# Scaling and transposing the next pair's queries one slot later, in a fused retention and feed-forward kernel

## The chip, the cores and the metric

The kernel runs on one core of a Trainium2 chip. The metric is device time in microseconds (us) of one execution; lower is better. Every engine (TensorE or PE, VectorE or DVE, ScalarE or ACT, GpSimd or POOL, SyncE or SP) has its own queue and works through it strictly in order; semaphores join them.

## The reference

Two blocks, one after the other, in float32.

```python
# retention: batch 4, 8 heads, 768 steps, head size 64
for t in range(S):
    state = gamma * state + k[:, :, t] (outer) v[:, :, t]
    y[:, :, t] = scale * q[:, :, t] @ state
x = y.transpose(0, 2, 1, 3).reshape(3072, 512)
# feed-forward: w_in 512 x 2048, w_out 2048 x 512 (given as float64)
h = x @ w_in
g = h * erf(softplus(h))
out = g @ w_out
```

## The kernel before

**Tokens.** The 3072 tokens are cut into 24 chunks of 128 (`j`), two to a group (`g`, 12 groups, `NG`). A *pair* is the two chunks `a = 2g+2` and `b = 2g+3`. Retention of a chunk is done in closed form: `begin` multiplies keys by queries (L566) and keys by values (L573) on PE, `states` masks and adds on DVE (L582, L593), `results` multiplies with states and values on PE (L611, L622) and copies to `xT` on ACT (L630), `crossed_sums` adds the rest on DVE (L641). `split_x` cuts a group's `xT` into three float32r parts, `x_hi` on ACT (L314), `x_lo` and `x_dif` on DVE (L315, L316).

**Preparing a pair.** Before a pair can begin, `load_pair` loads its values and keys (`v`, `kn`; four DMAs issued by POOL) and, in another layout, its keys and queries (`kb`, then `qb`; 16 DMAs each on SP, 128-byte rows). `prepare` is a generator of five steps:

1. DVE transposes `kb` into `kT` (L543),
2. DVE multiplies `qb` by the query scales (L538),
3. DVE transposes `qb` into `qT` (L543),
4. ACT scales the eight heads of the first chunk's `v` (L550, eight instructions),
5. ACT scales the eight heads of the second chunk's `v` (L550, eight more).

`(steps, prep, n)` runs the next `n` of them.

**Periods and slots.** From group 3 on, a period `g` has eight slots. In each slot PE computes one `pair_unit` (L720): a tile of 128 columns of `h` for two groups, 8 matmuls into a bank `a` (parts hi and lo) and then 4 into a bank `b` (part dif). Two pairs of banks take turns, `o0`/`o1` and `o2`/`o3`. The order of the work is written out by hand in `period`: one dictionary says what PE does ahead of a slot's unit (`begin` of both chunks ahead of slot 2, `results` ahead of slot 5), another what the other engines do in a slot, and `put` comes last in it: ACT copies bank `a` into `h` (L322), DVE adds bank `b` (L323), POOL stores `h` to memory (`hids`, L731). So a unit of slot n+2 can write its bank `a` only after L322 of slot n, and its bank `b`, two thirds into the unit, only after L323 of slot n.

**Conversion.** w_out comes as float64 words and is turned into float32 on DVE and ACT, piece by piece. POOL loads quarters of a piece into `raw` (L208), then a piece has five steps: `power` from the exponents (L230, and L1019 on ACT at the end of the slot), L244, L249, L253 (after it `raw` is free), L265 (after it POOL stores the piece, `wof`, L271). `(convert, n)` runs the next `n` steps.

**Buffers.** Nearly all of these tiles (`kb`, `qb`, `kT`, `qT`, `v`, `kn`, `xT`, `w`, `power`) come out of one pool of 34 equal buffers, `b4`; a load waits until the buffer that it was given is free. `h` and the masked scores `am` share a pool of six buffers, `b2`, so ACT can write an `h` only when the store of the `h` that last held its buffer has ended.

**After the periods** (groups 10 to 12 and the loop over `project`, L905) come the gate and the second product; their own order does not change.

The slots of a period as they stand in the loop:

Of the kernel before, what the change touches and what calls it, by code (L numbers as in the profile page):

```python
# [49 lines left out]
def kernel(  # L50
# [19 lines left out]
    NG = B * S // GT  # L70
# [460 lines left out]
    def prepare(j):  # L531


        for name, store, x in (("k", KT, KB[j]), ("q", QT, QB[j])):
            if name == "q":
                own = x.rearrange("p u (a d) -> p u a d", d=32)
                scale = kq_b[:, 1, :, j % NC : j % NC + 2].rearrange("p u c a -> p u (c a)")
                nc.vector.tensor_tensor(  # L538
                    own, own, scale[:, :, :, None].to_broadcast([P, HP, 8, 32]), op=ALU.mult
                )  # L540
                yield
            t = b4(name + "T", [HP, 2 * C])
            nc.vector.transpose(t.rearrange("p u t -> p (u t)"), x.rearrange("p u t -> p (u t)"))  # L543
            for i in range(2):
                store[j + i] = t[:, :, i * C : (i + 1) * C]
            yield
        for i in range(2):
            for h in range(H):
                x = V[j + i][:, h]
                nc.scalar.activation(x, x, AF.Copy, scale=kq_s[:, (j + i) % NC, 0, h : h + 1])  # L550
            yield
# [245 lines left out]
    prep = prepare(JPC + 2)  # L797
# [127 lines left out]
    def joined(at, to, g):  # L925

        a, b = 2 * g + 2, 2 * g + 3
        return {
            at: [(begin, a, ps_h), (begin, b, ps_r)],
            to: [(results, a, None, ps_h), (results, b, None, ps_r)],  # L930
        }
# [4 lines left out]
    def period(g, prep, next_prep):  # L936

        a, b = 2 * g + 2, 2 * g + 3
        one, two = partial(partial, unit), partial(partial, pair_unit)
        if g == G2:  # L940
            units = [one(g, n) for n in range(NPC // 2)]
            return units, {0: [(results, a), (results, b, None, ps_h)]}, {
                0: [(crossed_sums, a), (crossed_sums, b)],
                1: [(split_x, a, 2)],
                2: [(split_weights, 4)],
                3: [(steps, next_prep, 4)],
            }, range(4)
        if g < NG:
            units = [two(g - 1, ft) for ft in range(8 * (g % 2), 8 * (g % 2) + 8)]
        if g == G2 + 1:  # L950
            return units, joined(2, 5, g), {
                0: [(steps, prep)],
                1: [(split_weights, 5)],
                2: [(states, a), (states, b)],
                3: [(split_weights, 6)],
                4: [(split_weights, 7)],
                5: [(crossed_sums, a), (crossed_sums, b)],
                6: [(split_x, a, 2)],
                7: [(steps, next_prep, 4)],
            }, range(4)  # L960
        if g < NG - 2:
            return units, joined(2, 5, g), {
                0: [(steps, prep), (convert, 1)],
                1: [(convert, 2)],
                2: [(states, a), (convert, 1)],
                3: [(states, b), (convert, 1)],
                4: [(convert, 2 if g < 8 else 1)],
                5: [(crossed_sums, a), (crossed_sums, b)],
                6: [(split_x, a, 2)],
                7: [(steps, next_prep, 4)],  # L970
            }, LOADS.get(g, ())
        if g == NG - 2:
            return units, {1: [(begin, a)], 2: [(results, a)], 3: [(begin, b)], 5: [(results, b)]}, {
                0: [(steps, prep), (load_w_out, 0)],
                1: [(states, a), (load_w_out, 1)],
                2: [(crossed_sums, a), (split_w_out, 0)],
                3: [(states, b), (split_x, a)],
                4: [(split_w_out, 1), (load_hiddens, 0)],
                5: [(crossed_sums, b)],
                6: [(split_x, b), (softplus, 0), (load_w_out, 2)],  # L980
                7: [(erf, 0), (gated, 0)],
            }, ()
        if g == NG - 1:
            return units, {}, {
                0: [(split_g, 0), (split_w_out, 2), (load_w_out, 3)],
                1: [(split_g, 1), (load_hiddens, 1)],
                2: [(split_w_out, 3)],
                3: [(softplus, 1), (load_w_out, 4)],
                4: [(erf, 1)],
                5: [(split_w_out, 4), (load_w_out, 5)],  # L990
                6: [(gated, 1)],
                7: [(split_g, 2), (load_hiddens, 2)],
            }, ()
        return [one(NG - 1, n) for n in range(NPC // 2)], {}, {
            0: [(split_w_out, 5), (load_w_out, 6)],
            1: [(split_g, 3), (load_w_out, 7)],
            2: [(split_w_out, 6)],
        }, ()

    for g in range(G2, NG + 1):  # L1000
        pair = load_pair(2 * g + 4) if 2 * g + 4 < NJ else iter(())
        next_prep = prepare(2 * g + 4) if 2 * g + 4 < NJ else iter(())
        units, pe, other, loads = period(g, prep, next_prep)
        for i, work in enumerate(units):
            for f, *args in pe.get(i, ()):
                f(*args)
            put = work()
            steps(pair, 3)
            for part in itertools.islice(quarters, loads.count(i)):
                load_quarter(part)  # L1010
            if g == NG - 1 and i % 2:
                W.pop(NPC // 2 + i // 2)
            if g == NG:
                W.pop(i)
            for f, *args in other.get(i, ()):
                f(*args)
            put()
            while behind:
                behind.pop(0)()  # L1019
        prep = next_prep  # L1020
    split_w_out(7)

    for n in range(NG * NU):
        g, i = divmod(n, NU)
# [62 lines left out]
```

## Time and profile before

| What | Value |
|---|---|
| median of the runs | 614.31 us (614.19, 614.31, and one of 3471.9) |
| the profiled execution | 614.87 us, of it a span of 613.2 us in the profile |
| PE busy | 605.6 us, 99% of the span |
| DVE busy | 459.6 us, 75% |
| ACT busy | 390.6 us, 64% |
| POOL busy | 131.8 us, 21% |
| granted TensorE clock | full speed |
| chain that ended last | PE 98% |

Times in rows of the profile are in us from the start of the span. In a timeline a row gives start, duration, engine, line, operation, output and input, count, and in brackets how long the engine stood idle before it and what released it. In the chain of waits a row gives start, duration and what the end waited on at that time. The period of group 4 begins about 128 us into the span, that of group 9 about 261 us.

### The profile page before, as it was taken

How to read it: one execution, taken by the hardware profiler on the slowest of the kernel's cores; microseconds unless marked ns; L12 is line 12 of the kernel's file. 1: busy time of each engine (PE TensorE's matmuls, PEld its weight loads, DVE VectorE, ACT ScalarE, POOL GpSimd, SP SyncE). 2: the span in 40 equal slices, each digit the busy share in tenths (PEclk: the TensorE clock that was granted, in tenths of full speed). 3: DMA queues.
4: the chain of work that ended last, by engine and by line, in shares of the span. 5: the costliest groups of instructions: out<-in, count | busy, mean ns of one | idle time of the engine just before them, and what ended most of it. 6: DMA issues, size and time to landing. Idle time of an engine off the chain costs nothing.

```text
span 613.2 us, 13161 instructions
## 1 busy us (share of the span) xinstructions
PE 605.6 (99%) x5222; PEld 507.8 (83%) x5222; DVE 459.6 (75%) x581; ACT 390.6 (64%) x614; POOL 131.8 (21%) x228
## 2 busy tenths in 40 slices
PE   8999999999999999999999999999999999999997
PEld 7888889888888788888888988888888888888886
DVE  5899978796968779787758978686786768668640
ACT  3667446354451635435387699879789888988920
POOL 1086335443526255242112100000000000000000
PEclk9999999999999999999999999999999999999999
DMA  9999659977889896878435934325324333531300
GB/s 204 321 268 267 158 133 253 250 153 230 208 242 235 233 289 162 260 177 263 163 133 191 288 131 129 128 87 172 103 78 163 104 117 125 171 114 59 104 35 34
DMA packets 143949, 106.28 MB, mean 173 GB/s; under 512 B 103056, under 2 KB 123792, under 8 KB 143888
## 3 DMA queue, kind: packets, MB, share of 16 engines
q1 hardware_dynamic: 128160, 58.09, 37.0%
q0 software_dynamic: 15168, 47.21, 23.9%
q8 instruction: 41, 0.67, 0.5%
q10 hardware_dynamic: 560, 0.14, 0.1%
q14 instruction: 20, 0.16, 0.1%
HBM read 69.75 MB, written 35.65 MB: 172 GB/s over the span
## 4 chain that ended last, share of the span: by engine, by line
PE 98%; DMA 0%; DVE 0%; ACT 0%; issue 0%; DVEq 0%
PE o L720 31%; PE o L905 21%; PE r L905 11%; PE hp L905 11%; PE hp L665 9%; PE o L693 3%; PE hp L566 1%; PE hp L720 1%; PE r L720 1%; PE r L566 1%; PE r L611 1%; PE r L622 1%; PE r L573 1%; PE hp L611 1%; PE r L465 1%; PE o L504 1%
## 5 line engine op out<-in xcount | busy, mean ns | idle before, releaser
L322 ACT ACTIVATE h<-o 128x512 f32<-128x512 f32 x74 | 44.0, 597 | 100.7 <-PE o L720 84.1
L720 PE MATMUL o<-x_hi,w_hi 128*128 128x512 f32 x272 | 108.1, 397 | 0.0
L720 PE MATMUL o<-x_lo,w_lo 128*128 128x512 f32 x272 | 106.0, 390 | 0.0
L860 DVE TENSOR_TENSOR e<-hid,e 128x1024 f32<-128x1024 f32 x48 | 56.7, 1222 | 61.8 <-ACT e L850 61.8
L720 PE MATMUL o<-x_dif,w_dif 128*128 128x512 f32 x272 | 73.0, 390 | 1.3 <-DVE h L323 1.3
L323 DVE SCALAR_TENSOR_TENSOR h<-o,h 128x512 f32<-128x512 f32 x74 | 50.3, 682 | 27.5 <-ACT h L322 21.1
L731 POOL DMA_DIRECT2D hids<-h x72 | 39.3, 546 | 146.3 <-DVE h L323 125.5
L720 PEld LDWEIGHTS o<-x_dif,w_dif 128*128 128x128 f32 x272 | 50.9, 188 | 12.7 <-DVE h L323 2.1
L316 DVE SCALAR_TENSOR_TENSOR g_dif<-g_hi,g_lo 128x1024 fp32r<-128x1024 f32 x48 | 58.8, 1225 | 3.3
L720 PEld LDWEIGHTS o<-x_hi,w_hi 128*128 128x128 f32 x272 | 51.0, 188 | 11.5
L314 ACT ACTIVATE g_hi<-e 128x1024 fp32r<-128x1024 f32 x48 | 51.0, 1062 | 13.6 <-DVE e L860 11.6
L720 PEld LDWEIGHTS o<-x_lo,w_lo 128*128 128x128 f32 x272 | 51.1, 188 | 10.1
L315 DVE TENSOR_TENSOR g_lo<-e,g_hi 128x1024 fp32r<-128x1024 f32 x48 | 58.6, 1222 | 0.5
L665 PE MATMUL hp<-xT,w 128*128 128x256 f32 x256 | 57.2, 381 | 0.0
L665 PEld LDWEIGHTS hp<-xT,w 128*128 128x128 f32 x256 | 48.0, 190 | 6.6
L846 ACT ACTIVATE e<-hid 128x1024 f32<-128x1024 f32 x48 | 48.2, 1053 | 0.3
L850 ACT ACTIVATE e<-e 128x1024 f32<-128x1024 f32 x48 | 48.2, 1052 | 0.3
L905 PE MATMUL o<-w_hi,g_hi 128*128 128x512 f32 x120 | 46.7, 389 | 0.0
L905 PE MATMUL o<-w_lo,g_lo 128*128 128x512 f32 x120 | 46.7, 389 | 0.0
L905 PE MATMUL o<-w_dif,g_dif 128*128 128x512 f32 x120 | 46.7, 389 | 0.0
L550 ACT ACTIVATE v<-v,kq_s 128x64 f32<-128x64 f32 x144 | 36.2, 337 | 0.0
L846 ACT ACT_TABLE_LOAD x24 | 30.8, 1283 | 0.5
(201 smaller groups left out, 1267.5 us busy)
## 6 DMA issues: line engine op xcount, KB each, us to landing
hids<-h POOLq DMA_DIRECT2D x72, 256.0 KB, 3.9
hid<-hids SPq DMA_DIRECT2D x36, 512.0 KB, 4.6
raw<-in_moe_w_in_dram SPq DMA_DIRECT2D x32, 256.0 KB, 5.4
raw<-in_moe_w_out_dram POOLq DMA_DIRECT2D x32, 256.0 KB, 5.9
hid<-hid SPq DMA_DIRECT2D x12, 512.0 KB, 4.8
out_dram<-y SPq DMA_DIRECT2D x23, 256.0 KB, 2.3
kb<-in_k_dram SPq DMA_DIRECT2D x144, 32.0 KB, 2.9
v<-in_v_dram POOLq DMA_DIRECT2D x18, 256.0 KB, 6.2
```

The source lines that it names most:

```text
L314: nc.scalar.activation(hi, x, AF.Copy, scale=KEEP)
L315: nc.vector.tensor_tensor(lo, x, hi.bitcast(F32), op=ALU.subtract)
L316: nc.vector.scalar_tensor_tensor(dif, hi.bitcast(F32), Z, lo.bitcast(F32), op0=ALU.mult, op1=ALU.subtract)
L322: nc.scalar.activation(to, a, AF.Copy, scale=1 + 1 / Z)
L323: nc.vector.scalar_tensor_tensor(to, b, -1 / Z, to, op0=ALU.mult, op1=ALU.add)
L665: nc.tensor.matmul(HP_[ft][:, g], w[:, kk, ft % 2 * P : (ft % 2 + 1) * P], XC[g][:, kk], start=(kk == 0), stop=(kk == n_k - 1),)
L720: nc.tensor.matmul(to, W[n][i][:, kk * 2 * P + u * P : kk * 2 * P + (u + 1) * P], XR[i][:, at, kk], start=(kk == 0 and i == parts[0]), sto ...
L731: nc.gpsimd.dma_start(HID2[g][:, ft % 8], h)
L846: nc.scalar.activation(E[n], HID_[n], AF.Softplus)
L850: nc.scalar.activation(E[n], E[n], AF.Erf)
L860: nc.vector.tensor_tensor(E[n], HID_.pop(n), E[n], op=ALU.mult)
L905: nc.tensor.matmul(Y[g][t][x // 2], G[n][x][:, f, t * P : (t + 1) * P], W_OUT[ft // 2][x][:, ft % 2 * d_model : (ft % 2 + 1) * d_model], s ...
```

## The change

Of the five steps of `prepare`, only the first (the transpose of `kb`) stays in slot 7 of the period in front; steps 2 to 4, which scale and transpose the queries and scale the first chunk's values, join step 5 in slot 0 of the pair's own period. One `convert` step goes from slot 0 to slot 7 of the same period. It holds for the six hand-overs from period 3 to 4 up to period 8 to 9. At the hand-over from 9 to 10 the four steps stay in slot 7, and the conversion step is put behind them there. PE's instructions and their order stay as they were; SP and POOL issue the same DMAs, POOL in a slightly different order.

```diff
         if g == G2 + 1:
...
-                7: [(steps, next_prep, 4)],
+                7: [(steps, next_prep, 1)],
             }, range(4)
         if g < NG - 2:
             return units, joined(2, 5, g), {
-                0: [(steps, prep), (convert, 1)],
+                0: [(steps, prep, 4)],
                 1: [(convert, 2)],
                 2: [(states, a), (convert, 1)],
                 3: [(states, b), (convert, 1)],
                 4: [(convert, 2 if g < 8 else 1)],
                 5: [(crossed_sums, a), (crossed_sums, b)],
                 6: [(split_x, a, 2)],
-                7: [(steps, next_prep, 4)],
+                7: [(steps, next_prep, 1 if g < NG - 3 else 4), (convert, 1)],
             }, LOADS.get(g, ())
         if g == NG - 2:
...
-                0: [(steps, prep), (load_w_out, 0)],
+                0: [(steps, prep, 4), (load_w_out, 0)],
```

## The prediction

> **What bounds the kernel now.** I read the page first: the span, the busy shares, the chain that ended last.
>
> ```profile
> span 613.2 us, 13161 instructions
> ...
> PE 605.6 (99%) x5222; PEld 507.8 (83%) x5222; DVE 459.6 (75%) x581; ACT 390.6 (64%) x614; POOL 131.8 (21%) x228
> ...
> PE 98%; DMA 0%; DVE 0%; ACT 0%; issue 0%; DVEq 0%
> ```
>
> PE sets the time, and none of its work is touched. The change can only take away, or add, time in which PE stands still. So the next view is the waits of PE, and after it the busy time in stretches, cut where the chain shows `begin` of each pair (slot 2 of periods 4 to 9).
>
> ```profile
> PE o L720 <- DVE h L323: 1.3, 1, 1.3
> ```
>
> ```profile
> 134.08:160.36 26.28, 26.28 (x340) 21.80 (x343) 20.75 (x32) 11.88 (x30) 11.21 (x18) 1.00 0.77 203
> 160.36:186.66 26.30, 26.30 (x340) 21.49 (x343) 20.12 (x31) 11.79 (x30) 10.24 (x18) 1.00 0.88 232
> 186.66:214.61 27.95, 26.61 (x356) 21.73 (x359) 21.27 (x34) 12.61 (x31) 12.69 (x21) 1.00 0.94 250
> 214.61:240.92 26.31, 26.31 (x340) 21.79 (x342) 22.42 (x33) 12.01 (x30) 12.31 (x20) 1.00 0.82 226
> 240.92:267.02 26.10, 26.10 (x341) 21.57 (x343) 20.02 (x31) 11.89 (x30) 9.67 (x17) 1.00 0.82 216
> ```
>
> Columns: length of the stretch, busy PE, weight loads, DVE, ACT, POOL, granted clock, share of the DMA engines, GB/s. One stretch stands out: 27.95 us against about 26.2 in the others. It is the period of group 6 with the hand-over to 7, and its DMA share is the highest, 0.94. DVE is busy for about 80% of a period, so it has some 5 us to spare in each. The chain says where PE lost time; each row is the five units of slots 5, 6, 7, 0, 1, except that in the third hand-over it is broken.
>
> ```profile
> 146.53 13.82 PE o L720 x60
> ...
> 172.59 14.07 PE o L720 x60
> ...
> 199.16 12.93 PE o L720 x56
> ...
> 212.11 0.61 ACT h L322
> 212.72 0.65 DVE h L323
> ...
> 213.41 1.20 PE o L720 x4
> ...
> 227.06 13.87 PE o L720 x60
> 240.92 0.62 PE hp L566 x32
> ...
> 242.95 8.39 PE o L720 x36
> ...
> 253.15 13.87 PE o L720 x60
> ```
>
> Five units take 13.82 us when nothing holds them: 2.72 us each, and 0.2 more after a change of work; `begin` takes the 2.0 us from 240.92 to 242.95. At 199.16 they end at 214.61, 15.45 later: 1.63 lost. At 172.59: 0.25 lost. At 227.06 and 253.15: 0.05 each. Sum 1.98 us. That is all that the hand-overs of before hold for a gain. The wait itself stands in the unit of slot 1, whose last four matmuls (the row of 213.41) need the bank that L323 of slot 7 must have read. S below is the start of slot 0, 8.2 us after the start of such a row: 207.4 in the long hand-over.
>
> **Why that L323 is late.** DVE and ACT around the long hand-over:
>
> ```profile
> 200.16 0.69 DVE L230 TENSOR_SCALAR power<-raw 128x1024 uint32<-128x1024 uint32 x1 [3.09 <-DMA raw<-in_moe_w_out_dram]
> ...
> 207.24 0.68 DVE L323 SCALAR_TENSOR_TENSOR h<-o,h 128x512 f32<-128x512 f32 x1
> 207.84 1.24 DVE L543 STREAM_TRANSPOSE kT<-kb 128x1024 f32<-128x1024 f32 x1
> 210.27 1.23 DVE L538 TENSOR_TENSOR qb<-qb,kq_b 128x1024 f32<-128x1024 f32 x1 [1.20 <-DMA kb<-in_k_dram]
> 211.53 1.25 DVE L543 STREAM_TRANSPOSE qT<-qb 128x1024 f32<-128x1024 f32 x1
> 212.70 0.65 DVE L323 SCALAR_TENSOR_TENSOR h<-o,h 128x512 f32<-128x512 f32 x1
> ```
>
> ```profile
> 199.49 0.60 ACT L322 ACTIVATE h<-o 128x512 f32<-128x512 f32 x1 [5.37 <-DMA hids<-h]
> 200.90 1.15 ACT L1019 ACTIVATE power<-power,below 128x1024 uint32<-128x1024 uint32 x1 [0.81 <-DVE power L230]
> ...
> 205.18 2.01 ACT L550 ACTIVATE v<-v,kq_s 128x64 f32<-128x64 f32 x8
> 207.10 0.58 ACT L322 ACTIVATE h<-o 128x512 f32<-128x512 f32 x1
> 207.58 2.01 ACT L550 ACTIVATE v<-v,kq_s 128x64 f32<-128x64 f32 x8
> ```
>
> `put` of slot 7 had its ACT half done at 207.68. Its DVE half stood behind the transpose of `kb`, a wait of 1.20 us for a load (the row names `kb`, but L538 reads `qb` alone), the multiply and the transpose, and began at 212.70. The unit of slot 1 wants that bank two thirds into itself, at S + 2.72 + 1.8 = 211.9. The short loss of the hand-over from 5 to 6 goes back to the same wait, 1.85 us:
>
> ```profile
> 176.24 1.23 DVE L315 TENSOR_TENSOR x_lo<-xT,x_hi 128x1024 fp32r<-128x1024 f32 x1
> ...
> 182.33 1.23 DVE L538 TENSOR_TENSOR qb<-qb,kq_b 128x1024 f32<-128x1024 f32 x1 [1.85 <-DMA qb<-in_q_dram]
> ```
>
> SP's queue, loads of the pair after that:
>
> ```profile
> 180.51 7.96 SPq L159 DMA_DIRECT2D kb<-in_k_dram  x16
> 188.57 16.93 SPq L159 DMA_DIRECT2D qb<-in_q_dram  x16
> ```
>
> **The change part by part.** *Steps 2 and 3, to slot 0.* L538 and L543, 1.23 + 1.25 us and any wait for `qb`, go from ahead of L323 of slot 7 to behind it. In the long hand-over DVE then runs L543 of `kb` to 209.0, the conversion step that came into slot 7 (there L230, 0.69) to 209.7, and L323 to 210.4: 1.5 us before PE wants the bank. The 1.63, 0.25 and both 0.05 go. Late next is `qT`: L538 from 210.4, L543 to 212.9, and `begin` wants it at 199.16 + 13.82 = 213.0. Just in time. In a hand-over in which nothing is late:
>
> ```profile
> 233.74 1.23 DVE L543 STREAM_TRANSPOSE kT<-kb 128x1024 f32<-128x1024 f32 x1
> ...
> 239.59 1.21 DVE L265 SCALAR_TENSOR_TENSOR w<-w,power 128x1024 f32<-128x1024 f32 x1
> ```
>
> ```profile
> 234.62 0.60 ACT L322 ACTIVATE h<-o 128x512 f32<-128x512 f32 x1 [0.21 <-PE o L720]
> ```
>
> `kT` to 234.9, a conversion step (L230 0.69 to L265 1.21) to 236.1, L323 to 236.8, L538 and L543 to 239.3; `begin` at 240.92. Slack 1.6 us: price nothing, and what hides it is the unit of slot 1.
>
> *Step 4, to slot 0.* ACT scales sixteen heads in one go, twice 2.01 us less the overlap, 3.9 us, after L322 of slot 7. Behind it in ACT's queue stands L322 of slot 0, and DVE's L323 waits for that. In the quiet hand-over: 235.2 to 239.1, L322 to 239.7 instead of 237.9, L323 to 240.4. The unit of slot 2 wants both banks after `begin`, from 242.95; without `begin` as cover it would want them from 240.9, and even that is met. DVE stands still for about 1 us and takes it from its 5 us. The values, ready at 239.1, are wanted after the 0.62 us of L566, at 241.5. Price nothing.
>
> In the long hand-over ACT has more ahead of it: L1019 (1.15 us) belongs to the L230 that now stands in slot 7 and cannot start before 209.7. Scaling then ends at 214.8; the second chunk's values are wanted last in `begin`, some 1.6 us into it, at 214.6, and after L322 of slot 0, at 215.4, comes the unit of slot 2, which wants its bank at 215.0. Bounds: 0 if period 6 is less late than it was, 0.7 us (both waits and the signals between engines) if it is as late. What makes it late is L322 at 199.49, which waited 5.37 us for the store of the `h` that held its buffer. POOL issued the store of slot 0 at
>
> ```profile
> 191.42 0.55 POOL L731 DMA_DIRECT2D hids<-h  x1
> ```
>
> behind four loads of values and keys, and these behind the store of slot 7's `h`, so behind L323 of slot 7, which comes some 2 us earlier now. But a store slowed by full DMA engines stays slow. I take 0.5, nearer to the row as it stands.
>
> *The conversion step.* L230 of period 6 goes from slot 4, where it stood 3.09 us for `raw`, to slot 7. All other steps come one step later inside a period; the last L208 of a piece waits with them for L253, in period 5 for one slot. `raw` has periods to spare: nothing. At the hand-over from 9 to 10 slot 7 grows by one L265, 1.21:
>
> ```profile
> 289.74 0.65 DVE L323 SCALAR_TENSOR_TENSOR h<-o,h 128x512 f32<-128x512 f32 x1
> ...
> 293.61 1.07 PE L720 MATMUL o<-x_dif,w_dif 128*128 128x512 f32 x4
> ```
>
> L323 moves from 289.74 to 290.96 and ends at 291.6; PE wants its bank at 293.61. Nothing, 2 us to spare.
>
> *Buffers and queues.* The built program hands out the 34 buffers in another order. New `kb` of pairs 14, 16, 20 and 22 now takes over from an `xT`, last read by `x_lo`, and no longer from the `kb` in front. In period 5 that read ends at 177.5, the load started at 180.51: 3 us earlier. `qb` mostly takes over from an older `qb`, free only after step 3 in slot 0, at about S + 4; but SP gets to it only when 16 loads of `kb` are issued, 8 us after their start, so it does not wait. Whether the queries then land 3 us earlier (slack in the long hand-over grows, and the 0.5 falls to 0) or at the old time (0.7), the DMA shares of 0.88 and 0.94 leave open; the bounds hold both. By the Trainium skill ("DMA: Bandwidth & Descriptors", section "Issuing engines are not separate DMA queues") transfers of SP and POOL share the same 16 engines and interleave; by it an earlier issue under such load brings little, and the gain would be the lower end, 1.3.
>
> **Sum.** 1.98 gone, 0.5 new: 1.5 us less, bounds 1.3 and 2.0. Against the profiled execution: 614.87 - 1.5 = 613.4, span 611.7. The median of the runs lies 0.56 below that execution: 614.31 - 1.5 = **612.8 us**.
>
> **The rivals.** *Nothing gained, 614.3.* The loss is one of loads and stores, not of order: the queries land as late, and `begin` waits in place of the unit of slot 1. For: the loss sits in the stretch with the fullest DMA engines, and the slack of `begin` there is 0.1 us. Against: the same rows, with the loads as late as they were, leave 0.7 of the 1.98. It needs loads about 1 us later. 614.31, give or take 0.4.
>
> *Slower, by `begin` waiting for `qT` in slot 2.* L538 and L543 need 2.5 us and `begin` stands at S + 5.6, so it waits from the point where the queries land later than S + 3.1. Before, they landed at S + 1.5 (182.33 against 172.59 + 8.2) and at S + 2.9 (210.27 against 207.4). If the new order of buffers and loads made them land 3 us later, as much as I have them start earlier, these two wait 1.4 and 2.8: 4.2 - 1.98 = +2.2, 616.5 us. For: the gate of `kb` has changed in every pair. Against: the gates that I can date come earlier. For a loss of over 2%, 12.3 us (about what a measurement of this kernel can tell from no change), each of six hand-overs would have to lose 2.4 us. By the Trainium skill ("TensorE: Matmul & The Clock Gate", "Part 1: The HAM clock gate") PE falls to half speed after an idle window of about 3.4 us, which would make longer waits dearer; the stretch of 27.95 us, with a wait of 1.6, still shows 1.00.
>
> *A gain of over 2%* has no place: 1.98 is all there is.
>
> **How the numbers follow.** Forecast 0.62; nothing gained 0.20; slower 0.15, of it 0.03 over 2%; the rest, a gain beyond the bounds among it, 0.03. The forecast's own range is 612.3 to 613.2 with 0.1 of scatter beyond its bounds; for 8 in 10 I go from 612.0 to 615.2, which takes in the second case and the nearer part of the third. Faster by over 2% 0.01, within 2% 0.96, slower by over 2% 0.03.
>
> **What would show it.** Right: no wait of L720 on L323 among PE's waits; the stretch from 186.66 to 214.61 shrinks to about 26.8 and the one before it to 26.05, the others stay; L538 stands behind L323 on DVE without idle time; `kb` of pair 16 is issued near 177.5; ACT shows L550 x16. Wrong: L566 or L573 waiting for `qT` or `v`; L720 waiting for L322 of slot 0; a stretch of 27.3 us or more.

## The result and the profile after

The changed kernel ran in 612.92 us (median of 13 runs, 612.58 to 613.94). The ratio to the kernel before, run beside it, is 0.9973, with a 95% interval of 0.9964 to 0.9982: 1.7 us less, between 1.1 and 2.2 (the two medians, 614.87 and 612.92, differ by 1.95). That is a small change, well under 2%, and its interval leaves out zero. The profiled execution took 613.15 us (614.87 before).

The page of the changed kernel, span, busy time and chain:

```profile
span 611.4 us, 13214 instructions
...
PE 604.6 (99%) x5222; PEld 507.3 (83%) x5222; DVE 459.8 (75%) x581; ACT 390.3 (64%) x614; POOL 132.5 (22%) x228
...
PE 96%; SPq 2%; DMA 1%; ACT 0%; DVE 0%; issue 0%; DVEq 0%
```

The engines do nearly the same work; the span is 1.8 us shorter. PE's waits no longer have a row for L323; what is left lies at the start of the kernel, and these are its three longest rows:

```profile
PE o L417 <- POOL ident masks.py:199: 1.5, 1, 1.5
PE o L497 <- ACT kqT L459: 0.6, 1, 0.6
PE r L465 <- ACT kqT L459: 0.6, 2, 0.3
```

The chain, hand-overs 5 to 6, 6 to 7 and 7 to 8 (start, length, five units in a row):

```profile
172.88 13.82 PE o L720 x60
...
199.17 13.82 PE o L720 x60
213.00 0.62 PE hp L566 x32
...
225.45 13.82 PE o L720 x60
```

Where the rows before read 14.07, 15.45 (broken in three) and 13.87, all read 13.82. The same in stretches from `begin` to `begin` (length, busy PE, weight loads, DVE, ACT, POOL, granted clock, DMA share, GB/s):

```profile
160.66:186.71 26.05, 26.05 (x340) 21.57 (x343) 21.82 (x33) 11.79 (x30) 10.13 (x18) 1.00 0.88 219
186.71:213.00 26.29, 26.29 (x356) 21.81 (x359) 20.17 (x31) 12.31 (x30) 13.51 (x21) 1.00 1.02 281
```

26.30 became 26.05 and 27.95 became 26.29. From the first hand-over to the last, 1.98 us went; the part ahead of the first was 0.3 us longer in this execution (the units of period 2 begin at 90.87, before at 90.56). So the full 1.98 was gained, not 1.5. DVE and ACT in the long hand-over:

```profile
205.23 0.68 DVE L323 SCALAR_TENSOR_TENSOR h<-o,h 128x512 f32<-128x512 f32 x1
205.83 1.23 DVE L543 STREAM_TRANSPOSE kT<-kb 128x1024 f32<-128x1024 f32 x1
206.99 0.65 DVE L230 TENSOR_SCALAR power<-raw 128x1024 uint32<-128x1024 uint32 x1
207.66 0.69 DVE L323 SCALAR_TENSOR_TENSOR h<-o,h 128x512 f32<-128x512 f32 x1
208.55 1.23 DVE L538 TENSOR_TENSOR qb<-qb,kq_b 128x1024 f32<-128x1024 f32 x1 [0.19 <-DMA kb<-in_k_dram]
209.81 1.25 DVE L543 STREAM_TRANSPOSE qT<-qb 128x1024 f32<-128x1024 f32 x1
```

```profile
197.70 0.60 ACT L322 ACTIVATE h<-o 128x512 f32<-128x512 f32 x1 [3.56 <-DMA hids<-h]
...
207.68 1.16 ACT L1019 ACTIVATE power<-power,below 128x1024 uint32<-128x1024 uint32 x1 [0.38 <-DVE power L230]
208.74 3.92 ACT L550 ACTIVATE v<-v,kq_s 128x64 f32<-128x64 f32 x16
212.56 1.06 ACT L322 ACTIVATE h<-o 128x512 f32<-128x512 f32 x2
```

L323 of slot 7 ends at 208.35, 3.6 us before the last four matmuls of slot 1's unit, which need its bank, start at 211.93; before it began at 212.70. `qT` is ready at 211.06, 1.9 us ahead of `begin` at 213.00, where the prediction had it "just in time". All of period 6 runs ahead of what it was: L322 of slot 4 waits 3.56 us for its store, not 5.37.

### The profile page after: what moved, and what is told of

It is laid out like the page before. It is cut to its first block, busy times and chain, and to the rows that moved or that the text cites. A ratio compares the mean times of both kernels' runs of the same rounds, so it can differ in the third digit from the quotient of the medians.

```text
span 611.4 us, 13214 instructions
## 1 busy us (share of the span) xinstructions
PE 604.6 (99%) x5222; PEld 507.3 (83%) x5222; DVE 459.8 (75%) x581; ACT 390.3 (64%) x614; POOL 132.5 (22%) x228
## 4 chain that ended last, share of the span: by engine, by line
PE 96%; SPq 2%; DMA 1%; ACT 0%; DVE 0%; issue 0%; DVEq 0%
PE o L720 31%; PE o L905 21%; PE r L905 11%; PE hp L905 11%; PE hp L665 9%; PE o L693 3%; PE hp L566 1%; DMA raw<-in_moe_w_in_dram 1%; PE hp L720 1%; PE r L720 1%; PE r L566 1%; PE r L611 1%; SPq L136 1%; PE r L622 1%; PE r L573 1%; PE hp L611 1%
## 5 line engine op out<-in xcount | busy, mean ns | idle before, releaser
L720 PE MATMUL o<-x_hi,w_hi 128*128 128x512 f32 x272 | 108.0, 397 | 0.0
L322 ACT ACTIVATE h<-o 128x512 f32<-128x512 f32 x74 | 43.8, 595 | 98.7 <-PE o L720 89.3
L720 PE MATMUL o<-x_lo,w_lo 128*128 128x512 f32 x272 | 106.0, 390 | 0.0
L323 DVE SCALAR_TENSOR_TENSOR h<-o,h 128x512 f32<-128x512 f32 x74 | 50.5, 686 | 34.3 <-ACT h L322 24.8
L720 PE MATMUL o<-x_dif,w_dif 128*128 128x512 f32 x272 | 72.7, 389 | 0.0
L720 PEld LDWEIGHTS o<-x_hi,w_hi 128*128 128x128 f32 x272 | 51.0, 188 | 11.4
L720 PEld LDWEIGHTS o<-x_dif,w_dif 128*128 128x128 f32 x272 | 51.1, 188 | 10.6
L720 PEld LDWEIGHTS o<-x_lo,w_lo 128*128 128x128 f32 x272 | 51.1, 188 | 10.1
L550 ACT ACTIVATE v<-v,kq_s 128x64 f32<-128x64 f32 x144 | 35.6, 335 | 0.0
```

Of the source, the lines that this page charges most:

```text
L322: nc.scalar.activation(to, a, AF.Copy, scale=1 + 1 / Z)
L323: nc.vector.scalar_tensor_tensor(to, b, -1 / Z, to, op0=ALU.mult, op1=ALU.add)
L720: nc.tensor.matmul(to, W[n][i][:, kk * 2 * P + u * P : kk * 2 * P + (u + 1) * P], XR[i][:, at, kk], start=(kk == 0 and i == parts[0]), sto ...
```

## The experiments

The table gives, for every profiled execution, the time from the start of slot 5's unit to `begin`, from PE's timeline: five units, 13.82 when nothing is late. "Ratio" is the time over that of the kernel before, with its 95% interval. A row grows by a little more than the wait in it: before, PE waits 1.33 us for L323 and the row is 1.63 longer; a wait of 2.00 in the last kernel makes its row 2.30 longer.

| Kernel | 3-4 | 4-5 | 5-6 | 6-7 | 7-8 | 8-9 | ratio |
|---|---|---|---|---|---|---|---|
| before | 13.83 | 13.83 | 14.07 | 15.45 | 13.86 | 13.87 | 1 |
| the change | 13.83 | 13.83 | 13.83 | 13.83 | 13.83 | 13.82 | 0.9973 [0.9964, 0.9982] |
| queries alone | 13.83 | 13.82 | 13.82 | 13.87 | 13.87 | 13.87 | 0.9975 [0.9963, 0.9987] |
| conversion alone | 13.83 | 13.87 | 14.31 | 17.61 | 13.86 | 16.01 | 1.0093 [1.0071, 1.0115] |
| values alone | 13.82 | 13.82 | 13.82 | 16.69 | 13.83 | 13.82 | 0.9987 [0.9971, 1.0003] |
| steps, no conversion | 13.82 | 13.82 | 13.83 | 13.82 | 13.82 | 13.83 | 0.9963 [0.9950, 0.9976] |
| 6 to 7 alone | 13.83 | 13.82 | 14.04 | 13.87 | 13.87 | 13.82 | 0.9984 [0.9972, 0.9995] |
| 5 to 6 alone | 13.82 | 13.82 | 13.87 | 13.87 | 13.86 | 13.83 | 0.9971 [0.9959, 0.9982] |
| 6 to 7, steps only | 13.83 | 13.83 | 13.84 | 14.11 | 13.83 | 13.83 | one execution |
| store ahead of loads | 13.83 | 13.87 | 13.83 | 16.01 | 13.82 | 13.83 | 1.0023 [1.0004, 1.0042] |
| raw earlier | 13.83 | 13.87 | 14.69 | 13.83 | 13.87 | 13.83 | 0.9991 [0.9982, 1.0001] |
| copy first, slot 7 | 13.83 | 13.83 | 13.83 | 15.65 | 13.86 | 13.87 | 1.0090 [1.0060, 1.0120] |
| copy first, slot 0 | 14.54 | 14.52 | 14.57 | 14.52 | 14.68 | 14.53 | 1.0144 [1.0115, 1.0173] |
| late by copies | 16.12 | 17.60 | 14.08 | 16.13 | 17.93 | 16.41 | one execution |

### Which part of the change did it

In the next four edits, as in the change, the hand-over from 9 to 10 keeps its four steps in slot 7.

**The queries alone.** In `prepare` the first chunk's values come second, then the queries.

```diff
-                7: [(steps, next_prep, 4)],
+                7: [(steps, next_prep, 2)],
...
-                0: [(steps, prep), (convert, 1)],
+                0: [(steps, prep, 3), (convert, 1)],
...
-                7: [(steps, next_prep, 4)],
+                7: [(steps, next_prep, 2 if g < NG - 3 else 4)],
```

> Only steps 2 and 3 (DVE scales and transposes the queries) move to slot 0; the first chunk's values stay in slot 7 and the conversion step in slot 0. Theory 1 (order on DVE: L323 of slot 7 stood behind the queries): the whole 1.98 us is gone, the hand-over rows of the chain all read 13.82, no L720 waits for L323; 2.0 us less than before, ratio 0.997. Theory 2 (the conversion step: L230 waited 3.09 us for raw in slot 4 of period 6 and made the period late): the order alone brings at most the small 0.25 of the hand-over from 5 to 6, ratio 0.9995 to 1. Theory 3 (values on ACT: L322 of slot 7 stood behind eight L550): nothing, ratio 1.

**The conversion step alone.**

```diff
-                0: [(steps, prep), (convert, 1)],
+                0: [(steps, prep, 1)],
...
-                7: [(steps, next_prep, 4)],
+                7: [(steps, next_prep, 4), (convert, 1)],
```

> Only the conversion step moves from slot 0 to slot 7, behind the four preparing steps, which stay there. Theory 1: L323 of slot 7 now stands behind one step more: 1.2 us in the hand-over from 5 to 6 (loss 0.25 becomes about 1.4), 0.7 from 6 to 7 (1.63 becomes about 2.3), about 0.4 from 8 to 9, where 0.8 us were to spare; together 2 us more than before (0.7 to 3), ratio 1.003. Theory 2: period 6 is no longer late, 1 to 1.6 us less, ratio 0.998. Theory 3: nothing.

**The values alone.**

```diff
-                7: [(steps, next_prep, 4)],
+                7: [(steps, next_prep, 3)],
...
-                0: [(steps, prep), (convert, 1)],
+                0: [(steps, prep, 2), (convert, 1)],
...
-                7: [(steps, next_prep, 4)],
+                7: [(steps, next_prep, 3 if g < NG - 3 else 4)],
```

> Only step 4 (the first chunk's values, eight L550 on ACT) moves to slot 0; the queries stay in slot 7, the conversion step in slot 0. Theory 1: DVE's order is that of before, so the loss of 1.98 us stays, ratio 1 (0.3 us either way). Theory 2: nothing either. Theory 3: L322 of slot 7 no longer stands behind L550, 1 to 2 us less, ratio 0.997.

**All three steps, without the conversion.**

```diff
-                7: [(steps, next_prep, 4)],
+                7: [(steps, next_prep, 1)],
...
-                0: [(steps, prep), (convert, 1)],
+                0: [(steps, prep, 4), (convert, 1)],
...
-                7: [(steps, next_prep, 4)],
+                7: [(steps, next_prep, 1 if g < NG - 3 else 4)],
```

> The three preparing steps move as in the change, the conversion step stays in slot 0. Theory 1: 1.98 us less, ratio 0.997, all hand-over rows 13.82; and no L1019 stands ahead of the sixteen L550 in the hand-over from 6 to 7, so nothing new can be lost there. Theory 2: L230 stays in slot 4 of period 6 behind its load, the period stays late and the loss with it, ratio 0.9995 to 1.

Theory 1 holds: two instructions on DVE, L538 and L543, placed behind L323 instead of ahead of it, bring the whole gain; whoever has them has 13.82 to 13.87 in every row. The values alone bring nothing to the long hand-over (its wait is there, 1.84 us), and their interval holds 1. The conversion step is the odd one: beside the moved queries it costs nothing (0.9973 and 0.9963 overlap), without them it is dear. The direction was expected, the size not: 5.7 us of span, not 2. PE's waits and DVE there:

```profile
PE o L720 <- DVE h L323: 5.0, 3, 3.0
```

```profile
211.86 1.23 DVE L538 TENSOR_TENSOR qb<-qb,kq_b 128x1024 f32<-128x1024 f32 x1 [2.41 <-DMA qb<-in_q_dram]
213.12 1.25 DVE L543 STREAM_TRANSPOSE qT<-qb 128x1024 f32<-128x1024 f32 x1
214.28 0.65 DVE L230 TENSOR_SCALAR power<-raw 128x1024 uint32<-128x1024 uint32 x1
214.85 0.68 DVE L323 SCALAR_TENSOR_TENSOR h<-o,h 128x512 f32<-128x512 f32 x1
```

L538 waits 2.41 us for its load instead of 1.20, and the wait of 2.96 us that PE gets from it is followed by a slower clock, which is the subject of the last experiment.

### Why the long hand-over was late

**The hand-over from 6 to 7 alone, and the one from 5 to 6 alone.**

```diff
-                0: [(steps, prep), (convert, 1)],
+                0: [(steps, prep, 4), *([] if g == 6 else [(convert, 1)])],
...
-                7: [(steps, next_prep, 4)],
+                7: [(steps, next_prep, 1 if g == 6 else 4), *([(convert, 1)] if g == 6 else [])],
```

> The change at the hand-over from 6 to 7 alone, with period 6's conversion step (L230) from slot 0 chain's place to slot 7; all other hand-overs as before. Theory L (late work feeds on itself: L323 late in the hand-over from 5 to 6 makes stores and loads of period 6 late): period 6 stays as late as before, L322 waits about 5 us for its store, the 0.25 of the hand-over from 5 to 6 stays, and in the hand-over from 6 to 7 0 to 0.7 us are lost to the L1019 and the sixteen L550; 0.9 to 1.6 us less than before, ratio 0.998. Theory R (period 6 is late by its own loads, and the position of L230 decides): the wait of L322 falls below 4 us as in the changed kernel, the hand-over from 6 to 7 reads 13.82; 1.6 us less.

```diff
-                0: [(steps, prep), (convert, 1)],
+                0: [(steps, prep, 4), (convert, 1)],
...
-                7: [(steps, next_prep, 4)],
+                7: [(steps, next_prep, 1 if g == 5 else 4)],
```

> The three preparing steps move at the hand-over from 5 to 6 alone; the long hand-over from 6 to 7 and the conversion stay as before. Theory L: stores and loads of period 6 are issued some 3 us earlier, L322 waits about 2.8 us for its store and L230 about 0.5 for raw, the queries of pair 16 land before L538 asks for them, and the hand-over from 6 to 7 loses nothing (13.82 to 14.0) although nothing was changed in it; 1.7 to 1.9 us less than before, ratio 0.997. Theory R: only the 0.25 of its own hand-over goes, the 1.63 stays, ratio 0.9995.

Theory L holds. With 5 to 6 alone, the long hand-over, in which nothing was changed, reads 13.87 instead of 15.45, and the whole ratio is there. L322 of slot 4 in period 6 (ACT) and L230 (DVE):

```profile
197.58 0.60 ACT L322 ACTIVATE h<-o 128x512 f32<-128x512 f32 x1 [3.17 <-DMA hids<-h]
```

```profile
198.26 0.69 DVE L230 TENSOR_SCALAR power<-raw 128x1024 uint32<-128x1024 uint32 x1 [0.83 <-DMA raw<-in_moe_w_out_dram]
...
207.43 1.23 DVE L538 TENSOR_TENSOR qb<-qb,kq_b 128x1024 f32<-128x1024 f32 x1
```

L322 waits less for its store, L230 waits 2.3 us less for `raw`, and the queries are there when L538 asks. The way from one hand-over to the next shows in POOL's queue: the store of slot 7's `h` stands in it ahead of the loads of the next pair, and it waits for L323. POOL of the kernel before, then with 5 to 6 alone:

```profile
185.71 0.54 POOL L731 DMA_DIRECT2D hids<-h  x1 [5.01 <-PE o L720]
186.27 0.90 POOL L143 DMA_DIRECT2D v<-in_v_dram  x1
```

```profile
182.63 0.54 POOL L731 DMA_DIRECT2D hids<-h  x1 [1.36 <-DMA qb<-in_q_dram]
183.51 0.91 POOL L143 DMA_DIRECT2D v<-in_v_dram  x1 [0.34 <-DMA kb<-in_k_dram]
```

Before, POOL stands still for 5.01 us until just after the late L323 (184.76 to 185.41; the row names PE, but the store reads what L323 wrote), and the loads behind that store leave some 3 us later than with 5 to 6 alone, where L323 ends at 182.33. So the 0.25 us lost in this hand-over were only the visible end of a lateness that came back as 1.63 in the next. The 0.25 itself comes and goes: three runs of this section (6 to 7 alone, the same without the conversion, store ahead of loads) leave the hand-over from 5 to 6 as it was, and read 14.04, 13.84 and 13.83 there, while POOL waits 4.6 to 4.9 us for that store in all three.

With 6 to 7 alone, period 6 stays late (L322 of slot 4 comes 12.1 us after `begin`; before 12.9, with 5 to 6 alone 10.7) and the hand-over from 5 to 6 keeps 0.2, but the long one loses 0.05 and not the 0 to 0.7 of the prediction's new term. So a cure in either place is enough for the long hand-over. What the prediction left out shows in the next run.

**The same without moving the conversion.**

```diff
-                0: [(steps, prep), (convert, 1)],
+                0: [(steps, prep, 4), (convert, 1)],
...
-                7: [(steps, next_prep, 4)],
+                7: [(steps, next_prep, 1 if g == 6 else 4)],
```

> As the run with the hand-over from 6 to 7 changed alone, but with the conversion step left where it was (L230 with its L1019 in slot 4 of period 6). It tells what moving that step is worth in the long hand-over. If taking L230 and L1019 out of slot 4 let ACT and DVE catch up there: period 6 is later than in that run, L323 of slot 6 at about begin + 20.6 instead of + 18.7, L543 of qT ends 0.2 to 0.7 us ahead of begin instead of 1.5; the row still reads 13.82 to 14.0. If moving the step gives nothing: the same 1.5.

DVE there, and then DVE of the run with the conversion moved:

```profile
200.94 0.69 DVE L230 TENSOR_SCALAR power<-raw 128x1024 uint32<-128x1024 uint32 x1 [3.63 <-DMA raw<-in_moe_w_out_dram]
...
212.04 1.25 DVE L543 STREAM_TRANSPOSE qT<-qb 128x1024 f32<-128x1024 f32 x1
```

```profile
205.81 0.68 DVE L323 SCALAR_TENSOR_TENSOR h<-o,h 128x512 f32<-128x512 f32 x1
...
207.57 0.65 DVE L230 TENSOR_SCALAR power<-raw 128x1024 uint32<-128x1024 uint32 x1
208.14 0.68 DVE L323 SCALAR_TENSOR_TENSOR h<-o,h 128x512 f32<-128x512 f32 x1
209.42 1.22 DVE L538 TENSOR_TENSOR qb<-qb,kq_b 128x1024 f32<-128x1024 f32 x1 [0.60 <-DMA kb<-in_k_dram]
210.68 1.25 DVE L543 STREAM_TRANSPOSE qT<-qb 128x1024 f32<-128x1024 f32 x1
```

Without moving the conversion `begin` waits 0.22 us for `qT`, which I had expected 0.2 to 0.7 early, and the row reads 14.11; with it `qT` is ready 1.5 us early. L323 of slot 6 comes at `begin` + 21.2 and + 18.7. Two single executions, so the size is rough, but the direction was on record: L230 with its wait for `raw`, and the L1019 behind it on ACT, are lifted out of slot 4, where both engines then catch up.

**Which lateness: the store or the loads?**

```diff
             put = work()
-            steps(pair, 3)
+            if g != 6:
+                steps(pair, 3)
...
             put()
+            if g == 6:
+                steps(pair, 3)
```

> The kernel before, but in period 6 alone the loads of the next pair (values and keys on POOL, kb and qb on SP) are issued behind the store of the slot's h instead of ahead of it. Theory L: the store of slot 0 leaves about 3 us earlier, L322 waits 2 to 3.5 us instead of 5.4, L323 of slot 7 comes earlier and the 1.63 us of the hand-over from 6 to 7 falls to 0.5 or less; 1 to 1.6 us less than before, ratio 0.998. If the place of the store in POOL's queue does not matter (the DMA engines are full and the store ends when it ends): wait and loss stay, ratio 1.

```diff
-    LOADS = {4: (3, 4, 5, 6), 5: range(2, 8), 6: (0, 1, 4, 5, 6, 7), ...
+    LOADS = {4: (3, 4, 5, 6), 5: (2, 3, 4, 5, 6, 6, 7, 7), 6: (4, 5, 6, 7), ...
```

> The kernel before, with the two loads of raw that POOL issued in slots 0 and 1 of period 6 issued in slots 6 and 7 of period 5, so that L230 in slot 4 of period 6 does not wait for them. Theory A (the wait for raw in slot 4 is a cause of the lateness of its own): the 3.09 us of L230 go, L323 of slots 4 and 5 come 0.7 to 1.2 us earlier, the loss of 1.63 us falls to 0.3 to 1.0; ratio 0.999. Theory B (that wait hides behind L322, which waits for its store as long, and the queries land as late): the loss stays at 1.4 to 1.7, ratio 1.

With the store in front, L322 of slot 4 does not wait for a store at all, and still the long hand-over is worse, 16.01. ACT, then DVE:

```profile
196.18 0.60 ACT L322 ACTIVATE h<-o 128x512 f32<-128x512 f32 x1 [2.12 <-PE o L720]
```

```profile
199.73 0.69 DVE L230 TENSOR_SCALAR power<-raw 128x1024 uint32<-128x1024 uint32 x1 [3.02 <-DMA raw<-in_moe_w_out_dram]
...
210.77 1.23 DVE L538 TENSOR_TENSOR qb<-qb,kq_b 128x1024 f32<-128x1024 f32 x1 [2.13 <-DMA qb<-in_q_dram]
```

So the place of the store was not the cause that I took it for: theory L's price for it is wrong, and with the loads of `raw` and of the queries still late the hand-over stays long. (The queries' load was issued 5.6 us later here, at 194.19 against 188.57, so this run cannot price the store alone.) With `raw` loaded earlier the long hand-over is clean, 13.83, although L322 of slot 4 still waits 4.99 us for its store; this is the better evidence that the wait for the store does not decide. But the hand-over from 5 to 6 now loses 0.87, because the queries of that pair land later (L538 waits 2.43 us for them; 1.43 to 1.85 in the kernels that leave that hand-over as it was). That the two loads moved into period 5 delay them there would fit; no run shows that step. Theory A, with a bill that it did not foresee.

### The rival made to happen

```diff
             put = work()
...
+            first = i == 0 and G2 + 1 < g < NG - 1
+            if first:
+                put()
             for f, *args in other.get(i, ()):
                 f(*args)
-            put()
+            if not first:
+                put()
```

> The changed kernel, with the queries and values of slot 0 behind that slot's copy (L322, L323) instead of ahead of it. This makes the rival of the prediction happen, begin waiting for qT: L323 of slot 0 cannot start before PE has ended the unit, S + 2.9, L538 and L543 follow to about S + 6.1, and begin stands at S + 5.6. By the sum of the prediction (2.5 us from the release to qT) each of six hand-overs loses 0.5 to 0.7 us, L566 waits for L543, the rows read about 14.4, together 3 to 4 us more than the changed kernel and 1 to 2 more than the kernel before, ratio 1.002. If the slack of 1.6 us of the prediction was larger than worked out: no wait, ratio 0.997.

The changed kernel with this edit. PE's waits:

```profile
PE hp L566 <- DVE qT L543: 3.9, 6, 0.8
PE o L720 <- issue: 2.8, 2, 1.8
```

The price of the rival was right: six waits, 0.65 us each on average, rows of 14.5. The total was not: about 9.5 us over the changed kernel, of it 4.4 in these rows and most of the rest behind the second row, two stalls in periods 5 and 8 for which the trace has no releaser (1.2 and 3.7 us of those stretches, the second with half clock behind it).

```diff
+            if i == 7 and g < NG - 2:
+                put()
             for f, *args in other.get(i, ()):
                 f(*args)
-            put()
+            if not (i == 7 and g < NG - 2):
+                put()
```

> The kernel before with one thing turned round: in slot 7 the copy of the slot's tile (L322, L323 and the store) comes ahead of the four preparing steps, which stay in slot 7; the conversion stays in slot 0. Theory 1 (order on DVE): L323 of slot 7 waits for PE alone, the whole 1.98 us goes, every hand-over row 13.82 to 13.87; kT and qT follow behind it and are ready some 1 us ahead of begin (S + 4.6 against S + 5.6); ratio 0.997. If the slot in which the queries are prepared matters in itself, or kT now comes too late for begin: L566 waits, 14 or more in the rows, ratio 0.999 or above.

The kernel before with this edit. The expectation failed: 0.9% slower. PE's waits and SP's queue:

```profile
PE hp L566 <- DVE qT L543: 3.5, 2, 1.8
PE o L720 <- issue: 1.6, 1, 1.6
```

```profile
183.18 12.50 SPq L159 DMA_DIRECT2D kb<-in_k_dram  x16
195.78 12.82 SPq L159 DMA_DIRECT2D qb<-in_q_dram  x16
```

L323 is early in every hand-over, but L543 of `kT` has come behind it too, and that is what frees the buffer for the next `kb` (the chain of this run goes from L543, which ends at 183.17, to that load): it starts at 183.18 instead of 180.51, and in the long hand-over the queries land so late that `begin` waits 1.76 us and the row, 15.65, is no shorter than before. The second such wait is at 9 to 10, where `begin` stands ahead of slot 1 and not of slot 2, which my expectation overlooked. Together with the second row, a stop of 1.60 us in period 7 that the trace does not explain, this makes up most of the 3.9 us by which the span is longer. Order on DVE is thus not all: here the transpose of `kb` had to stay ahead, with only the queries behind.

### What a wait of PE costs

```diff
-                7: [(steps, next_prep, 4)],
+                7: [(steps, next_prep, 4), (late, {4: 16, 5: 7, 6: 5, 7: 19, 8: 14}.get(g, 0))],
...
+    def late(n):
+        for _ in range(n):
+            nc.vector.tensor_copy(kq_b, kq_b)
```

(and 14 copies in period 3)

> The kernel before, with DVE copies of a constant table onto itself put behind the preparing steps in slot 7: 14, 16, 7, 5, 19 and 14 of them in the six hand-overs, about 0.2 us each, so that PE waits for L323 by different amounts in one run. Theory P (a wait costs its own length): each hand-over row is longer than 13.82 by its wait, and the granted clock stays at 1.00 for waits under 3 us; from 0.8 to 2.5 us a hand-over, 6 to 10 us in all. Theory C (a wait of somewhat under 2 us can already halve the granted clock for some 3.5 us, as behind the wait of 1.84 us in the run with the values moved alone, but not behind the 1.90 of the run with the conversion moved alone): waits from 1.3 to 2 us show half clock in some hand-overs and full clock in others, and each half-clock stretch adds up to 1.8 us.

A copy took 257 ns, and the six hand-overs lost 15.3 us, not 6 to 10. Two of the waits, 2.00 and 2.01 us long, from PE's timeline, and the clock behind each, from the stretches:

```profile
135.35 1.19 PE L720 MATMUL o<-x_dif,w_dif 128*128 128x512 f32 x4 [2.00 <-DVE h L323]
...
220.88 1.20 PE L720 MATMUL o<-x_dif,w_dif 128*128 128x512 f32 x4 [2.01 <-DVE h L323]
```

```profile
133.30:135.35 2.05, 0.06 (x1) 0.00 (x0) 1.91 (x7) 0.00 (x0) 0.00 (x0) 1.00 0.40 65
135.35:138.50 3.15, 3.15 (x117) 2.63 (x117) 3.12 (x5) 1.63 (x2) 2.88 (x4) 1.00 0.54 137
220.90:222.50 1.60, 1.60 (x35) 1.14 (x39) 1.60 (x3) 0.00 (x0) 1.36 (x2) 0.98 0.52 120
222.50:226.00 3.50, 3.50 (x98) 3.29 (x89) 3.47 (x7) 0.00 (x0) 2.75 (x5) 0.52 0.93 192
```

Behind the first the granted clock (third column from the right) stays at 1.00, behind the other it falls to half for some 3.5 us. Theory C holds for waits of about 2 us; the shorter ones come from the other runs. Over all runs: half clock behind stops of PE of 1.76 (copy first in slot 0), 1.84, 2.01, 2.25, 2.57, 2.96 and 3.46 us; full clock behind 0.99, 1.33 (the kernel before), 1.60, 1.76 (copy first in slot 7, twice), 1.89, 1.90 and 2.00. In the run with the values alone:

```profile
211.00:213.50 2.50, 0.66 (x4) 0.21 (x2) 2.46 (x4) 0.74 (x2) 0.00 (x0) 1.00 0.64 131
213.50:217.00 3.50, 3.50 (x65) 2.65 (x69) 3.50 (x5) 0.00 (x0) 2.51 (x4) 0.53 0.67 160
```

A wait of 1.84 us cost 3.6 there: the hand-over is 2.87 too long, and the stretch behind `begin` 0.77.

## Why the prediction was right, and where it was not

**What bounds the kernel, and what there was to gain: right.** PE alone; 1.98 us in the hand-overs; all of it in units that waited for L323 of slot 7. The signs named for it came: no wait of L720 for L323, 26.05 for the stretch in front, 26.29 for the long one (I had 26.8), L538 behind L323 (0.19 us of idle time), `kb` of pair 16 issued at 177.79, L550 x16.

**The mechanism, steps 2 and 3 behind L323: right,** shown by the queries alone.

**Step 4 and the quiet hand-overs, priced at nothing: right.** The slack of `begin` that covered them showed its edge when the queries went one copy further back: six waits of 0.65.

**The new term of 0.5 us in the long hand-over: wrong, it measured 0.** The step that failed stands in "Step 4, to slot 0": L1019 "belongs to the L230 that now stands in slot 7 and cannot start before 209.7". L1019 started at 207.68 in the changed kernel and at 208.25 in the run with 6 to 7 alone. I added L230 and its L1019 to slot 7 and left slot 6 as late as before; but the same edit takes them, and the 3.09 us wait for `raw`, out of slot 4, and the edit one hand-over earlier takes out the lateness itself. Either alone is enough: L323 of slot 6 starts 20.7 us after `begin` in the kernel before, 18.7 with 6 to 7 alone, 18.6 with 5 to 6 alone and 18.6 with both. For the same reason `qT`, "just in time" by my sum, was 1.9 us early. The bound of 0 was there, "if period 6 is less late than it was"; I took the other end for the wrong reason, that "a store slowed by full DMA engines stays slow". The store is not what decides (with `raw` earlier it is waited for 4.99 us and the row is clean), and the lateness was fed by the hand-over in front (5 to 6 alone).

**The loads.** In period 6 of the changed kernel the issue of the queries ended where it did before, at 205.5, though `kb` started 2.7 us earlier; they were ready 1.8 us earlier, counted from `begin` (L538 at 21.9 against 23.7). The Trainium skill ("DMA: Bandwidth & Descriptors", "Issuing engines are not separate DMA queues") has the DMAs of all issuing engines run on the same 16 DMA engines and interleave; I had concluded from it that an earlier issue under such load brings little. The trace agrees with that conclusion on the end of the issue and not on the result, since the gain came whole and not at its lower end.

**The time: 612.8 predicted, 612.92 measured.** The nearness is partly luck: the gain in the rows was 0.5 more than forecast, and the runs of the kernel before lay 0.6 above the three that I had been shown (614.87 against 614.31). A ratio of 0.9964 to 0.9982 does not tell 1.5 from 1.98; the rows of the chain do.

**The rivals.** "Nothing gained" did not come: the queries landed earlier, not later. The slower one had its price right, and did not come for the reason given, gates that move earlier; with the copy first in slot 7 a gate moved 2.7 us later, and `begin` waited 1.76 us.

**The clock.** The prediction gave the rule of the Trainium skill ("TensorE: Matmul & The Clock Gate", "Part 1: The HAM clock gate"), half speed after an idle window of about 3.4 us. Here 1.76 us were enough once and 2.00 were not always, so the measurement decides against the rule as a limit. (The wait in the stretch of 27.95 us was 1.33 us long, not 1.6; 1.63 is what the row lost.) The same section calls the window free-running; two waits of equal length that end differently agree with that, though no run here shows the window itself.

## What to carry to other kernels

When an engine in strict order has a stall, look for the instruction that frees another engine's buffer and see what stands ahead of it with a wait of its own; move that behind it, and leave ahead whatever frees a buffer for the next load. A small loss in one period may be the cause of a large one in the next, so try the cure one place earlier than where the loss shows. And when work is moved, take it out of its old place in the sum as carefully as it is put into the new one.

## What the runs showed that I had not expected

A wait of PE of about 2 us may cost its length or nearly twice that, and nothing in these runs says beforehand which: half clock for some 3.5 us, up to 1.7 us more. That accounts for the upper end of the scatter of the kernel before. Of the 67 executions of it that ran beside the experiments, 57 took 613.4 to 616.2 us at a mean granted clock of 0.999 or 1.000, and ten took 616.5 to 617.4 us at 0.996 or 0.997. One stretch of 3.5 us at half clock lowers the mean over 613 us to 0.997, and the run with the values alone, whose trace has such a stretch, shows 0.996. All 13 executions of the changed kernel, 612.6 to 613.9 us, are at 0.999 or 1.000. So the change also takes away the occasional dearer execution. In which stretch those ten lost their clock no trace shows, since the profiled execution of the kernel before ran at full clock.

PE stood still three times without a releaser in the trace, 0.99 and 1.76 us in one run (copy first in slot 0) and 1.60 in another (copy first in slot 7), each time with the DMA engines full (shares of 1.06 to 1.21 during the stop). In each case the queue that reads the program's own instructions began a block of 16 KB 0.8 to 1.6 us before the stop, one of 41 in the whole execution. A wait for instructions would fit, but no run tests it, and what PE waited for stays open.
